# Transposing attention outputs and mask rows by DMA in place of TensorE, in a fused attention and MoE kernel

## The chip, the cores and the metric

The kernel runs on one core of one Trainium2 chip. The metric is the device time of one execution in microseconds (us). The profile is one further execution, and its span is about 1.7 us shorter than the time that the same execution is given. Engine names in the profile: PE is TensorE (matmuls and transposes), PEld its weight loads, DVE is VectorE, ACT is ScalarE, POOL is GpSimd, SP is SyncE, which here only issues DMAs.

## The reference

Four batches of eight heads, sequence 768, head dimension 64. Each query attends causally to its own block of 64 keys and to the best-scoring other blocks (gate: query times the mean key of a block). The concatenated heads then go through two dense layers with a tanh-approximated GELU.

```python
k_rep = k.reshape(B, H, n_blocks, block, D).mean(axis=3)
gate_scores = np.einsum('bhsd,bhnd->bhsn', q, k_rep)          # causal blocks only
top_idx = np.argsort(gate_scores, axis=-1)[..., -3:]          # plus the own block -> mask
attn = softmax(where(mask & causal, scale * q @ k.T, -1e9)) @ v
x = attn.transpose(0, 2, 1, 3).reshape(B * S, H * D)          # 3072 x 512
out = gelu_tanh(x @ w_in) @ w_out                             # 512 -> 2048 -> 512
```

## The kernel before

Two heads form a pair; there are 16 pairs, 4 to a batch. For each pair a preparation stage turns K and Q into columns (on PE for pairs 0 to 4, on DVE from pair 5 on), computes the gate, selects blocks, and writes mask rows under the Q columns. The head stage then computes scores, exponentials and the product with V. Each batch ends with two dense products: `s1` (w_in, then GELU) and `s2` (w_out).

The order of the instructions on every engine is fixed when the kernel is built: a planner in the kernel simulates the engines with guessed durations and writes the instructions down in the order that comes out. It decides the order only; at run time semaphores (counters that one engine raises and another waits for) decide the moment.

```python
# guesses: {engine: us}; "DMA" is the time a load takes to land, SP the issue
go = add({SP: 0.2}, emit_t if dve else emit, [free_sd.get(...)], prio=10 * p)
ld[key, p] = add({"DMA": 4.5 if dve else 2.0}, lambda _: None, [go, at_least], ...)

# mask rows of a pair: madd[i] is [128, 10, 32]: 5 query chunks x 2 heads, 32 columns each;
# one transpose takes one chunk of both heads (128 x 64)
def mask(_):
    mk16 = plan.buf["mk", p].bitcast(FP16)
    for c in range(1, NC):                                   # NC = 6
        nc.tensor.transpose(
            mk16[0:64, c * 128:(c + 1) * 128],
            madd[i][:, 2 * (c - 1):2 * c, :].rearrange("p a b -> p (a b)"), ident16)
m = add({PE: 0.27 * slow}, mask, [sel], pr, takes=("pre", ("mk", p)))
# ... then two copies of 12 x 640 from PSUM into qT16[i][h][64:76, 128:S] (DVE or ACT)

# output of a pair: six 128x128 transposes on PE, then a copy PSUM -> xT
def ot_e(_):
    oT16 = plan.buf["oT", p].bitcast(FP16)
    for c in range(NC):
        nc.tensor.transpose(
            oT16[:, c * 128:(c + 1) * 128],
            T["xn", p][:, c].rearrange("p h d -> p (h d)"), ident16)
ot = add({PE: 0.32 * slow}, ot_e, norms, base + 50, takes=("pre", ("oT", p)))

# 110 idle matmuls of lowest priority that keep PE warm in the first batch
z = const.tile([128, 512], FP16)
nc.vector.memset(z, 0.0)
for n in range(110):
    def emit(_, n=n):
        nc.tensor.matmul(plan.buf["warm", n][:, 0:256], z[:, 0:128],
                         z[:, 0:256], start=True, stop=True)
    add({PE: 0.107}, emit, [], 1e6, ...)
```

The softmax here doesn't subtract the row's maximum and nothing guards it: scores larger than these inputs give would overflow.

## Time and profile before

| | before |
|---|---|
| median time | 294.3 us |
| span of the profile | 291.4 us |
| PE busy | 279.3 us |
| first w_in matmul of batch 0 | 49.8 us |
| from there to the end of the span | 241.6 us |

The profiled execution took 293.1 us, 1.2 us under the median, and the table's last rows belong to it.

From the page of the kernel before: the span, the busy time of each engine, two rows of the span in 40 slices (tenths busy), and the engines of the chain of work that ended last.

```profile
span 291.4 us, 5960 instructions
...
PE 279.3 (96%) x2330; PEld 173.8 (60%) x2330; DVE 144.0 (49%) x448; ACT 191.5 (66%) x252; POOL 48.0 (16%) x119
...
PE   7998899899999999999999999999999999999994
...
DMA  9999999999999966865822110200000101100111
...
PE 80%; ACT 13%; DVE 3%; issue 2%; POOL 1%; ACTq 0%; DVEq 0%
```

PE is busy nearly everywhere and is 80% of the chain. The DMA engines are full for the first 14 of 40 slices and nearly idle in the second half. To see how tight PE is after the first batch, here are the busy times by stretch (start:end, length, busy, number of instructions, granted clock, DMA share, GB/s):

```profile
core 0: us, PE busy (x), PEclk, DMA share, GB/s
49.80:287.50 237.70, 235.34 (x1867) 1.00 0.45 84
119.00:146.00 27.00, 26.82 (x180) 1.00 0.71 126
```

From the first w_in matmul to the end of the last w_out product PE idles 2.4 us of 237.7. PE time that is taken out there should come off the span, unless something new makes PE wait. This is from the list of the w_in line's instructions (durations ns min/median/max, first and last start in us):

```profile
L629 PE MATMUL wide_85<-xT_555,w_in_102 x64: 270/324/390, 49.8 to 73.7; 128*128 128x512 f16 x32, 128*128 128x256 f16 x32
...
L629 PE MATMUL wide_86<-xT_3108,w_in_102 x64: 272/326/379, 247.2 to 266.6; 128*128 128x512 f16 x32, 128*128 128x256 f16 x32
```

What the two kinds of transposes take is read from the timeline of PE (start, duration, engine, line). The durations overlap, because matmuls are pipelined, so the cost of a group is the distance between its start and the next group's start. First a mask, then an output:

```profile
136.28 0.49 PE L629 MATMUL wide_86<-xT_1428,w_in_102 128*128 128x512 f16 x2
136.70 0.47 PE L472 MATMUL bank_88<-ident_96,madd_121 128*64 128x128 f16 x5
137.10 1.15 PE L629 MATMUL wide_86<-xT_1428,w_in_102 128*128 128x512 f16 x6
```

```profile
229.51 0.50 PE L600 MATMUL bank_88<-ident_96,xn_3219 128*128 128x128 f16 x6
229.85 0.38 PE L571 MATMUL bank_89<-v_126,at_0_1_3261 128*128 128x65 f16 x7
```

The mask group takes 0.40 us to the next start. In front of it another 0.1 us is lost: w_in matmuls in a row take 1.30 us for eight (in the list of the chain), so the two ahead should need 0.325 us, and the gap is 0.42. The output group takes 0.34 us.

### The profile page before, as it was taken

How to read it: one execution, taken by the hardware profiler on the slowest of the kernel's cores; microseconds unless marked ns; L12 is line 12 of the kernel's file. 1: busy time of each engine (PE TensorE's matmuls, PEld its weight loads, DVE VectorE, ACT ScalarE, POOL GpSimd, SP SyncE). 2: the span in 40 equal slices, each digit the busy share in tenths (PEclk: the TensorE clock that was granted, in tenths of full speed). 3: DMA queues.
4: the chain of work that ended last, by engine and by line, in shares of the span. 5: the costliest groups of instructions: out<-in, count | busy, mean ns of one | idle time of the engine just before them, and what ended most of it. 6: DMA issues, size and time to landing. Idle time of an engine off the chain costs nothing.

```text
span 291.4 us, 5960 instructions
## 1 busy us (share of the span) xinstructions
PE 279.3 (96%) x2330; PEld 173.8 (60%) x2330; DVE 144.0 (49%) x448; ACT 191.5 (66%) x252; POOL 48.0 (16%) x119
## 2 busy tenths in 40 slices
PE   7998899899999999999999999999999999999994
PEld 6776667575666655656646665666557644665441
DVE  4787873138578878673676978850024410000000
ACT  3667869557799695676789976376799921664111
POOL 7023224000043220000024430000034400000000
PEclk9999999999999999999999999999999999999999
DMA  9999999999999966865822110200000101100111
GB/s 171 219 213 197 190 171 174 199 170 146 168 159 175 163 133 146 177 127 97 128 43 64 58 38 37 74 0 0 2 36 2 40 36 72 38 0 2 72 72 72
DMA packets 115836, 29.75 MB, mean 102 GB/s; under 512 B 110176, under 2 KB 112224, under 8 KB 115808
## 3 DMA queue, kind: packets, MB, share of 16 engines
q1 hardware_dynamic: 113216, 25.18, 47.7%
q0 software_dynamic: 2592, 4.19, 8.4%
q8 instruction: 18, 0.29, 0.4%
q14 instruction: 10, 0.08, 0.1%
HBM read 27.26 MB, written 6.29 MB: 115 GB/s over the span
## 4 chain that ended last, share of the span: by engine, by line
PE 80%; ACT 13%; DVE 3%; issue 2%; POOL 1%; ACTq 0%; DVEq 0%
PE wide_86 L629 14%; PE wide_85 L629 14%; PE bank_88 L659 7%; PE bank_87 L659 7%; PE bank_90 L659 6%; PE bank_89 L659 6%; PE wide_85 L533 5%; PE wide_86 L533 4%; PE bank_89 L430 3%; PE bank_90 L571 2%; PE bank_89 L571 1%; PE bank_90 L430 1%; PE bank_88 L430 1%; PE bank_87 L571 1%; PE bank_88 L600 1%
## 5 line engine op out<-in xcount | busy, mean ns | idle before, releaser
L629 PEld LDWEIGHTS <-w_in_102 128*128 128x128 f16 x512 | 49.7, 99 | 34.0 <-issue 1.8
L659 PEld LDWEIGHTS <-gT_3446 128*128 128x128 f16 x96 | 9.4, 98 | 11.2
L659 PEld LDWEIGHTS <-gT_2781 128*128 128x128 f16 x96 | 9.1, 97 | 8.0
L694 PEld LDWEIGHTS <-z 128*128 128x128 f16 x110 | 10.9, 105 | 4.2 <-DVE bmask L164 1.3
L659 PEld LDWEIGHTS <-gT_1883 128*128 128x128 f16 x96 | 8.8, 98 | 7.6
L629 PE MATMUL wide_85<-xT_555,w_in_102 128*128 128x512 f16 x64 | 12.4, 326 | 1.0 <-ACT gT_986 L642 0.6
L629 PE MATMUL wide_86<-xT_1428,w_in_102 128*128 128x512 f16 x64 | 12.4, 326 | 0.2 <-ACT gT_1883 L642 0.2
L659 PEld LDWEIGHTS <-gT_986 128*128 128x128 f16 x96 | 8.5, 98 | 6.7
L629 PE MATMUL wide_85<-xT_3108,w_in_102 128*128 128x512 f16 x64 | 12.2, 326 | 0.0
L629 PE MATMUL wide_86<-xT_555,w_in_102 128*128 128x512 f16 x64 | 12.2, 326 | 0.0
L629 PE MATMUL wide_86<-xT_2319,w_in_102 128*128 128x512 f16 x64 | 12.0, 326 | 0.0
L629 PE MATMUL wide_85<-xT_2319,w_in_102 128*128 128x512 f16 x64 | 11.9, 326 | 0.0
L629 PE MATMUL wide_86<-xT_3108,w_in_102 128*128 128x512 f16 x64 | 11.7, 326 | 0.0
L629 PE MATMUL wide_85<-xT_1428,w_in_102 128*128 128x512 f16 x64 | 11.7, 326 | 0.0
L504 ACT ACT_TABLE_LOAD x8 | 10.3, 1283 | 0.9 <-PEq L746 0.8
L642 ACT ACTIVATE gT_986<-wide_85 128x768 f16<-128x768 f32 x8 | 6.5, 810 | 5.2 <-PE wide_85 L629 5.2
L190 DVE COPY osb_0_3000<-bank_89 128x512 f32<-128x512 f32 x1 | 0.7, 692 | 18.4 <-PE bank_89 L659 18.4
L659 PE MATMUL bank_90<-w_out_103,gT_2781 128*128 128x512 f16 x32 | 9.7, 379 | 0.0
L642 ACT ACTIVATE gT_986<-wide_86 128x768 f16<-128x768 f32 x8 | 6.5, 808 | 4.6 <-PE wide_86 L629 4.6
L694 PE MATMUL bank_88<-z 128*128 128x256 f16 x33 | 8.9, 290 | 0.3 <-ACT kT_1_107 L188 0.3
L642 ACT ACTIVATE gT_2781<-wide_86 128x768 f16<-128x768 f32 x8 | 6.5, 810 | 3.8 <-PE wide_86 L629 3.8
L642 ACT ACTIVATE gT_3446<-wide_86 128x768 f16<-128x768 f32 x8 | 6.5, 810 | 3.7 <-PE wide_86 L629 3.7
(947 smaller groups left out, 697.4 us busy)
## 6 DMA issues: line engine op xcount, KB each, us to landing
w_in_102<-in_moe_w_in_dram POOLq DMA_DIRECT2D x1, 2048.0 KB, 14.3
w_out_103<-in_moe_w_out_dram POOLq DMA_DIRECT2D x1, 2048.0 KB, 17.3
k_sd_135<-in_k_dram SPq DMA_DIRECT2D x2, 192.0 KB, 3.0
q_sd_142<-in_q_dram SPq DMA_DIRECT2D x2, 192.0 KB, 3.7
v_sd_147<-in_v_dram SPq DMA_DIRECT2D x2, 192.0 KB, 4.3
k_sd_152<-in_k_dram SPq DMA_DIRECT2D x2, 192.0 KB, 4.6
q_sd_157<-in_q_dram SPq DMA_DIRECT2D x2, 192.0 KB, 4.6
v_sd_162<-in_v_dram SPq DMA_DIRECT2D x2, 192.0 KB, 4.5
```

The costliest lines, as they stand in the source:

```text
L190: nc.vector.tensor_copy(out=out, in_=in_)
L430: nc.tensor.matmul(gt[:, (c - 1) * 24:c * 24], T["qT32", p][:, c * 128:(c + 1) * 128], T["ksb", p].rearrange("p h n -> p (h n)"), start=Tr ...
L504: nc.scalar.activation(out=t, in_=bmask[:, 0, 0:1], func=AF.Exp if key[0] == "exp" else AF.Gelu_apprx_tanh, bias=0.0, scale=1.0)
L533: nc.tensor.matmul(st[:, x:e], kT16[i][h][0:76, s0:s0 + 128], qT16[i][h][0:76, s0 + (x - cb):s0 + (e - cb)], start=True, stop=True)
L571: nc.tensor.matmul(pvv[:, qc, 0:65], at[:, cb + (qc - jc) * 128: cb + (qc - jc + 1) * 128], v16[i][:, jc, h, :], start=(gi == 0 and jc == ...
L600: nc.tensor.transpose(oT16[:, c * 128:(c + 1) * 128], T["xn", p][:, c].rearrange("p h d -> p (h d)"), ident16)
L629: nc.tensor.matmul(hps[:, u:e], w_in16[:, ci, f * 128:(f + 1) * 128], T["xT", b][:, ci, u:e], start=(ci == 0), stop=(ci == HP - 1))
L642: nc.scalar.activation(out=T["gT", b][:, f, :], in_=plan.buf["hps", b, f][:, 0:S], func=AF.Gelu_apprx_tanh, bias=0.0, scale=1.0)
L659: nc.tensor.matmul(plan.buf["ops", b, ti], T["gT", b][:, f, ti * 128:(ti + 1) * 128], w_out16[:, f, :], start=(f == 0), stop=(f == NF - 1))
L694: nc.tensor.matmul(plan.buf["warm", n][:, 0:256], z[:, 0:128], z[:, 0:256], start=True, stop=True)
```

## The change

The intent: PE is the bottleneck and the DMA engines are idle in the second half, so let them do the transposes. Output transposes go to DMA from pair 6 on (10 pairs), mask transposes from pair 8 on (8 pairs). Earlier pairs, in the stretch where the loads fill the DMA engines, stay on PE. The mask tile doubles to 64 columns per head, so that a chunk of both heads is a block of 128x128, and the two heads' mask rows come out at partitions 0 and 64 (before: 0 and 32). To make room, one kT32 buffer and two constant tiles go, and the warm-up matmuls take the identity matrix in place of a zeroed tile. The core of the diff:

```diff
-        madd.append(persist.tile([128, NG, 32], FP16, name=f"madd_{i}"))
+        madd.append(persist.tile([128, NG, 64], FP16, name=f"madd_{i}"))
...
+    def by_xbar(p):
+        return p >= 2 * HP                     # HP = 4: pair 8 on
...
+            T["E16"] = E16 = E32[0:12].bitcast(FP16)[:, 0:S]   # E32 is a kT32 buffer
...
-                    mk16[0:64, c * 128:(c + 1) * 128],
+                    mk16[:, c * 128:(c + 1) * 128],
...
+        def mask_dma(_):
+            T["mT", p] = hd.tile([128, S - 128], FP16, tag="mT", name=f"mT_{p}")
+            nc.sync.dma_start_transpose(
+                out=T["mT", p].rearrange("p (c q) -> p c q", q=128),
+                in_=madd[i].rearrange("p g n -> p (g n)"))
+        if by_xbar(p):
+            go = add({SP: 0.1}, mask_dma, [sel], pr)
+            m = add({"XBAR": 2.5}, lambda _: None, [go], pr)
+        else:
+            m = add({PE: 0.27 * slow}, mask, [sel], pr, takes=("pre", ("mk", p)))
...
+            nc.sync.dma_start_transpose(
+                out=T["xT", b][:, hp, :].rearrange("p (c q) -> p c q", q=128),
+                in_=T["xn", p].rearrange("p c h d -> p (c h d)"))
+        if p >= HP + 2:                        # pair 6 on
+            go = add({SP: 0.1}, ot_dma, norms, base - 20)
+            xts.setdefault(b, []).append(
+                add({"XBAR": 2.5}, lambda _: None, [go], base - 20))
...
-        z = const.tile([128, 512], FP16)
-        nc.vector.memset(z, 0.0)
+        z = ident16.unsqueeze(1).to_broadcast([128, 2, 128])
-                nc.tensor.matmul(plan.buf["warm", n][:, 0:256], z[:, 0:128], z[:, 0:256], ...)
+                nc.tensor.matmul(plan.buf["warm", n][:, 0:256], ident16, z, ...)
```

More of the change, by code (lines that the diff above doesn't have):

```diff
@@ L36 @@
     LAT = {"PE": 0.2, "ACT": 0.19, "DVE": 0.14, "POOL": 0.1, "SP": 0.1,
-           "DMA": 0.1, "NONE": 0.0}
+           "DMA": 0.1, "XBAR": 0.1, "NONE": 0.0}
     WINDOW = 0.03
@@ L148 @@
     hd = ctx.enter_context(tc.tile_pool(name="hd", bufs=3))
+    hd2 = ctx.enter_context(tc.tile_pool(name="hd2", bufs=2))
     atp = ctx.enter_context(tc.tile_pool(name="atp", bufs=7))
@@ L251, in e16 @@
         def e16(_):
-            T["E16"] = const.tile([12, S], FP16, name="E16")
-            E16 = T["E16"]
+            E32 = hd2.tile([128, S], FP32, tag="kT32", name="E32")
+            T["E16"] = E16 = E32[0:12].bitcast(FP16)[:, 0:S]
             nc.gpsimd.memset(E16, MASKVAL)
@@ L340, in emit @@
             def emit(_):
-                T[key + "T32", p] = hd.tile([128, S], FP32, tag=key + "T32",
-                                            name=f"{key}T32_{p}")
+                T[key + "T32", p] = (hd if key == "q" else hd2).tile(
+                    [128, S], FP32, tag=key + "T32", name=f"{key}T32_{p}")
                 nc.vector.transpose(
@@ L349, in pre @@
             t = add({DVE: 0.83}, tr("k"),
-                    [ld["k", p], last.get(p - 3, {}).get("pre")], pr)
+                    [ld["k", p], last.get(p - 2, {}).get("k32")], pr)
             free_sd["k", p] = t
@@ L392, in pre @@
         ksb = add({DVE: 0.1}, ksb_m, ksr, pr)
+        last.setdefault(p, {})["k32"] = add({"NONE": 0.0}, lambda _: None,
+                                            kcs + ksr, pr)
         def wq_t(a):
@@ L472, in mask @@
                 nc.tensor.transpose(
-                    mk16[0:64, c * 128:(c + 1) * 128],
+                    mk16[:, c * 128:(c + 1) * 128],
                     madd[i][:, 2 * (c - 1):2 * c, :].rearrange(
                         "p a b -> p (a b)"), ident16)
-        m = add({PE: 0.27 * slow}, mask, [sel], pr, takes=("pre", ("mk", p)))
         def mc(h):
             def emit(eng):
+                src = (T["mT", p] if by_xbar(p)
+                       else plan.buf["mk", p].bitcast(FP16)[:, 128:S])
                 copy(eng, qT16[i][h][64:76, 128:S],
-                     plan.buf["mk", p].bitcast(FP16)[
-                         32 * h:32 * h + 12, 128:S])
-            return emit
+                     src[64 * h:64 * h + 12, :])
+            return emit
+        def mask_dma(_):
+            T["mT", p] = hd.tile([128, S - 128], FP16, tag="mT",
+                                 name=f"mT_{p}")
+            nc.sync.dma_start_transpose(
[5 more added lines that the diff above has]
+        else:
+            m = add({PE: 0.27 * slow}, mask, [sel], pr,
+                    takes=("pre", ("mk", p)))
         mcs = [add({DVE: 0.4, ACT: 0.6}, mc(h), [m, old.get("s")], pr)
                for h in range(2)]
-        add({"NONE": 0.0}, lambda _: None, mcs, pr, gives=[("mk", p)])
+        add({"NONE": 0.0}, lambda _: None, mcs, pr,
+            gives=[] if by_xbar(p) else [("mk", p)])
         rdy[p] = [kcs[0::2] + [q16s[0], mcs[0], c_E["fill", i]],
@@ L602, in ot_e, with ot_dma @@
                     T["xn", p][:, c].rearrange("p h d -> p (h d)"), ident16)
+        def ot_dma(_):
+            if ("xT", b) not in T:
+                T["xT", b] = xtp.tile([128, HP, S], FP16, tag="xT",
+                                      name=f"xT_{b}")
+            nc.sync.dma_start_transpose(
[5 more added lines that the diff above has]
+                add({"XBAR": 2.5}, lambda _: None, [go], base - 20))
+            last.setdefault(p, {}).update(
+                {"k": st, "s": st, "v": pvs[-1]})
+            return
         ot = add({PE: 0.32 * slow}, ot_e, norms, base + 50,
@@ L689, in warm @@
     def warm():
-        z = const.tile([128, 512], FP16)
-        nc.vector.memset(z, 0.0)
+        z = ident16.unsqueeze(1).to_broadcast([128, 2, 128])
         for n in range(110):
             def emit(_, n=n):
-                nc.tensor.matmul(plan.buf["warm", n][:, 0:256], z[:, 0:128],
-                                 z[:, 0:256], start=True, stop=True)
+                nc.tensor.matmul(plan.buf["warm", n][:, 0:256], ident16, z,
+                                 start=True, stop=True)
             add({PE: 0.107}, emit, [], 1e6, takes=("warm", ("warm", n)),
```

## The prediction

> **What bounds the kernel now.** TensorE (PE). The page gives PE 279.3 us busy of a 291.4 us span, and the chain that ended last is 80% PE and 13% ScalarE. Read by stage (busy time of each engine in each stretch): from 56 to 287.6 us PE is busy 230.3 of 231.6 us, so it hardly ever waits there; VectorE and ScalarE have room (about half and two thirds busy). Wherever the attention heads wait for ScalarE's exponentials, the second MoE product (w_out) of the previous batch fills PE, and that filler is never used up: it ends at 118.7, 185.5 and 247 us, while the last head of each batch is normalised at about 112.8, 173.5 and 234.3 us. So PE time taken out after about 56 us should come off the span almost one for one; waits shorter than the filler cost nothing. Before 56 us the chain is VectorE, ScalarE and loads, and PE runs warm-up matmuls.
>
> **What is removed, from the timeline of PE.** An output transpose (6 transposes) takes 0.34 us from its first start to the next instruction (229.51 to 229.85). Ten pairs: 3.4 us. A mask transpose (5) takes 0.40 us (136.70 to 137.10) plus about 0.1 us before its first weight load ("issue" gaps of 0.3 us on the weight-load row), so 0.5 us. Eight pairs: 4.0 us. The mask pairs that stay get 128 columns in place of 64; their weight loads (110 ns against 98 ns for 128 columns) and that gap may shrink: 4 x 0.1 = 0.4 us after 56 us. Sum: 7.8 us, all on the PE chain. Also gone are ten PSUM copies of 0.56 us (VectorE) or 0.80 us (ScalarE), and PSUM bank holds; off the chain, so worth little.
>
> **What is added.** 18 DMA transposes of 160 to 192 KB on the SP queue. Plain transfers of 96 to 192 KB here take 2.9 to 4.5 us to land. The Trainium skill (VectorE: DVE Perf Modes, "The three transpose paths") gives 1309 ns for a 128x128 transpose through the DMA crossbar; six blocks in one DMA I estimate at 3 to 8 us with that page's figure. No run here shows it yet. Masks have over 10 us of slack: they are made a stage before the heads that use them. Outputs of pairs 11 and 15 have 12 to 13 us of filler. The tight one is pair 7: its xT is needed about 6 us after its normalisation, at 99% DMA share (DMA row, 76 to 119 us). I allow 0.7 us for a stall there and for reshuffled static order. The third kT32 buffer that goes, and the memset of a wider mask tile, should stay hidden.
>
> **Prediction.** 294.3 - 7.8 + 0.7 = 287.2 us, range 285.0 to 290.5. Faster by over 2% (below 288.4): 0.68; within 2%: 0.29; slower: 0.03.
>
> **What would show each step right.** PE instructions fall by 100 (2330 to 2230) and PE busy time by some 7 us; PE still over 96% busy from 56 us on; no output transposes on PE after batch 0 but for pairs 4 and 5; the DMA transposes land within 8 us; the first w_in matmul of batch 1 waits under 1 us for xT. The w_in stretches start progressively earlier: by about 2 us at the third, 7 us at the fourth.
>
> **What would make it wrong.** DMA transposes of 10 us and more, so that w_in matmuls wait for xT; transposes waiting in the SP queue behind output stores or loads (or holding loads up behind them); contention that delays loads between 76 and 144 us; a static order of instructions, planned with 2.5 us per transpose, that is unlucky where the real latency differs; warm-up or first-batch work that starts later.

## More of the kernel before

The start of the kernel turned out to matter. Its timeline (all engines):

```profile
1.30 0.39 PE L694 MATMUL bank_87<-z 128*128 128x256 f16 x1 [1.30 <-DVE bmask L164]
...
2.04 0.91 DVE L161 CAST ident_96<-ident_91 128x128 f16<-128x128 f32 x1 [0.65 <-POOL ident_91 masks.py:199]
...
5.36 0.49 PE L313 MATMUL bank_90<-ident_91,k_sd_135 128*128 128x128 f32 x3
```

The zeroed tile (its memset starts at 0.97 us) is ready early. The identity, which GpSimd and VectorE prepare, is cast only by 2.95 us (2.04 + 0.91). The first warm-up matmul starts at 1.30 us, and 23 of them stand ahead of the first K transpose on PE's queue.

## The result, and the profile after

| | before | after |
|---|---|---|
| median time | 294.29 us | 287.25 us |
| runs | 294.07 to 294.37 | 286.02 to 288.27 |
| ratio | | 0.976 (95% interval 0.972 to 0.980) |

Ratios are the mean time of one kernel's fast runs over that of the other's fast runs of the same rounds, so not quite the ratio of the medians. The change is faster by 2.4%. The runs of the changed kernel spread over 2.2 us, those of the kernel before over 0.3 in these rounds (0.9 to 1.4 in later ones). The profile below is of the slowest of the four runs of the changed kernel, and the profile before is of a fast one, so the two spans differ by 4.9 us where the medians differ by 7.0.

The page of the changed kernel, same lines:

```profile
span 286.5 us, 5770 instructions
...
PE 271.4 (95%) x2230; PEld 169.7 (59%) x2230; DVE 141.7 (49%) x442; ACT 186.6 (65%) x247; POOL 48.6 (17%) x119
...
PE   5988988899999999998999999999999999999994
...
DMA  9999999999997886897872536313011321000111
...
PE 79%; ACT 6%; DVE 6%; DMA 4%; issue 2%; POOL 1%; SPq 0%; ACTq 0%; DVEq 0%; POOLq 0%
```

PE lost 100 instructions and 7.9 us of busy time. The DMA row is fuller in the second half. DMA has entered the chain with 4%. Busy time by stretch, from the first w_in matmul and for the w_in stretch of batch 1:

```profile
core 0: us, PE busy (x), PEclk, DMA share, GB/s
52.50:282.70 230.20, 226.79 (x1767) 1.00 0.53 99
119.00:146.00 27.00, 25.48 (x160) 1.00 0.87 142
```

PE now idles 3.4 us in its main stretch, 1.5 of them between 119 and 146 us, where it idled 0.2 before. The w_in line of the changed kernel:

```profile
L665 PE MATMUL wide_88<-xT_556,w_in_105 x64: 270/324/381, 52.5 to 76.3; 128*128 128x512 f16 x32, 128*128 128x256 f16 x32
...
L665 PE MATMUL wide_89<-xT_3033,w_in_105 x64: 272/326/379, 242.4 to 261.8; 128*128 128x512 f16 x32, 128*128 128x256 f16 x32
```

Batch 0's w_in product begins 2.7 us **later** than before (52.5 against 49.8), the last batch's 4.8 us earlier. So the stretch from the first w_in matmul to the end of the span fell from 241.6 us to 234.0, by 7.6 us, and the start gave part of that back. The transposes' landing, from the list of DMA issues:

```profile
xT_1429<-xn_1724 SPq DMA_TRANSPOSE x1, 2.8
mT_1834<-madd_112 SPq DMA_TRANSPOSE x1, 3.8
mT_1932<-madd_118 SPq DMA_TRANSPOSE x1, 4.0
```

The last columns are the count and the us to landing. Over all 18, masks land 2.4 to 4.2 us after the issue, outputs 2.7 to 4.4. The plan had 2.5. In the Trainium skill (VectorE: DVE Perf Modes, "The three transpose paths") one 128x128 transpose by DMA takes 1309 ns; here five or six of them in one DMA land after some 3 us, so well under that figure for each.

Two places lose time. The first is the start (timeline, all engines):

```profile
2.05 0.91 DVE L162 CAST ident_99<-ident_94 128x128 f16<-128x128 f32 x1 [0.83 <-POOL ident_94 masks.py:199]
...
3.01 0.39 PE L729 MATMUL bank_90<-ident_99 128*128 128x256 f16 x1 [3.01 <-DVE ident_99 L162]
...
7.89 0.77 PE L317 MATMUL bank_93<-ident_94,k_sd_136 128*128 128x128 f32 x3
```

The warm-up matmuls now wait for the identity, which GpSimd makes and VectorE casts by 3.0 us. The first K transpose stands behind 23 of them and starts at 7.89 us in place of 5.36. The second is the batch-1 w_in stretch, again in the timeline of all engines:

```profile
126.38 0.28 DVE L463 SCALAR_TENSOR_TENSOR madd_118<-sel_1918,ownm_195 128x120 f16<-128x120 f32 x1
...
127.09 1.52 SPq L495 DMA_TRANSPOSE mT_1932<-madd_118  x1
...
131.13 0.72 ACT L189 COPY qT_1_114<-mT_1932 12x640 f16<-12x640 f16 x1 [1.20 <-DMA mT_1932<-madd_118]
131.13 0.32 DVE L191 COPY qT_0_113<-mT_1932 12x640 f16<-12x640 f16 x1 [3.58 <-DMA mT_1932<-madd_118]
...
133.46 0.70 PE L665 MATMUL wide_88<-xT_1429,w_in_105 128*128 128x512 f16 x3 [1.14 <-ACT gT_1865 L678]
```

The mask of pair 9 is written by 126.7 us, issued at 127.1 and lands at 131.1. VectorE has its mask copy next in order and stands still for 3.58 us; ScalarE has the other copy ahead of GELUs, so these come late and PE waits 1.14 us for one. No score of pair 9 is computed before 154 us, so nothing needed this mask soon. What needed the engines was the work queued behind the copies.

### The profile page after: what moved, and what is told of

The parts are those of the page before. It is cut to its first block, busy times and chain, and to the rows that moved or that the text cites. A ratio compares the mean times of both kernels' runs of the same rounds, so it can differ in the third digit from the quotient of the medians.

```text
span 286.5 us, 5770 instructions
## 1 busy us (share of the span) xinstructions
PE 271.4 (95%) x2230; PEld 169.7 (59%) x2230; DVE 141.7 (49%) x442; ACT 186.6 (65%) x247; POOL 48.6 (17%) x119
## 4 chain that ended last, share of the span: by engine, by line
PE 79%; ACT 6%; DVE 6%; DMA 4%; issue 2%; POOL 1%; SPq 0%; ACTq 0%; DVEq 0%; POOLq 0%
PE wide_88 L665 13%; PE wide_89 L665 13%; PE bank_90 L695 8%; PE bank_92 L695 8%; PE bank_91 L695 7%; PE wide_88 L554 6%; PE wide_89 L554 5%; PE bank_93 L695 3%; PE bank_93 L592 2%; PE bank_93 L437 2%; PE bank_92 L437 2%; PE bank_91 L437 2%; PE bank_90 L592 1%; DMA mT_1932<-madd_118 1%; DMA mT_1834<-madd_112 1%
## 5 line engine op out<-in xcount | busy, mean ns | idle before, releaser
L665 PEld LDWEIGHTS <-w_in_105 128*128 128x128 f16 x512 | 50.0, 99 | 35.4 <-issue 2.8
L695 PEld LDWEIGHTS <-gT_3363 128*128 128x128 f16 x96 | 9.4, 98 | 11.2
L729 PEld LDWEIGHTS <-ident_99 128*128 128x128 f16 x110 | 11.4, 109 | 5.8 <-DVE ident_99 L162 3.0
L695 PEld LDWEIGHTS <-gT_2720 128*128 128x128 f16 x96 | 9.1, 97 | 8.2
L695 PE MATMUL bank_92<-w_out_106,gT_987 128*128 128x512 f16 x48 | 13.6, 379 | 0.0
L695 PEld LDWEIGHTS <-gT_1865 128*128 128x128 f16 x96 | 9.0, 98 | 7.5
L665 PE MATMUL wide_88<-xT_556,w_in_105 128*128 128x512 f16 x64 | 12.4, 325 | 1.0 <-ACT gT_987 L678 0.6
L665 PE MATMUL wide_88<-xT_1429,w_in_105 128*128 128x512 f16 x64 | 11.9, 325 | 1.1 <-ACT gT_1865 L678 1.1
L695 PEld LDWEIGHTS <-gT_987 128*128 128x128 f16 x96 | 8.7, 99 | 6.8
L665 PE MATMUL wide_88<-xT_3033,w_in_105 128*128 128x512 f16 x64 | 12.2, 326 | 0.0
L665 PE MATMUL wide_89<-xT_556,w_in_105 128*128 128x512 f16 x64 | 12.2, 326 | 0.0
L665 PE MATMUL wide_88<-xT_2290,w_in_105 128*128 128x512 f16 x64 | 12.0, 325 | 0.0
L665 PE MATMUL wide_89<-xT_3033,w_in_105 128*128 128x512 f16 x64 | 11.7, 326 | 0.0
L665 PE MATMUL wide_89<-xT_1429,w_in_105 128*128 128x512 f16 x64 | 11.7, 326 | 0.0
L665 PE MATMUL wide_89<-xT_2290,w_in_105 128*128 128x512 f16 x64 | 11.7, 326 | 0.0
L525 ACT ACT_TABLE_LOAD x8 | 10.3, 1283 | 0.9 <-PEq L781 0.8
L729 PE MATMUL bank_90<-ident_99 128*128 128x256 f16 x24 | 7.2, 308 | 3.1 <-DVE ident_99 L162 3.0
L678 ACT ACTIVATE gT_987<-wide_88 128x768 f16<-128x768 f32 x8 | 6.5, 811 | 5.1 <-PE wide_88 L665 4.9
L678 ACT ACTIVATE gT_2720<-wide_88 128x768 f16<-128x768 f32 x8 | 6.5, 810 | 5.0 <-PE wide_88 L665 5.0
L695 PE MATMUL bank_91<-w_out_106,gT_2720 128*128 128x512 f16 x32 | 9.7, 379 | 0.0
L695 PE MATMUL bank_91<-w_out_106,gT_1865 128*128 128x512 f16 x32 | 9.7, 379 | 0.0
L678 ACT ACTIVATE gT_987<-wide_89 128x768 f16<-128x768 f32 x8 | 6.5, 809 | 4.7 <-PE wide_89 L665 4.7
```

What stands on the lines that cost most here:

```text
L525: nc.scalar.activation(out=t, in_=bmask[:, 0, 0:1], func=AF.Exp if key[0] == "exp" else AF.Gelu_apprx_tanh, bias=0.0, scale=1.0)
L665: nc.tensor.matmul(hps[:, u:e], w_in16[:, ci, f * 128:(f + 1) * 128], T["xT", b][:, ci, u:e], start=(ci == 0), stop=(ci == HP - 1))
L678: nc.scalar.activation(out=T["gT", b][:, f, :], in_=plan.buf["hps", b, f][:, 0:S], func=AF.Gelu_apprx_tanh, bias=0.0, scale=1.0)
L695: nc.tensor.matmul(plan.buf["ops", b, ti], T["gT", b][:, f, ti * 128:(ti + 1) * 128], w_out16[:, f, :], start=(f == 0), stop=(f == NF - 1))
L729: nc.tensor.matmul(plan.buf["warm", n][:, 0:256], ident16, z, start=True, stop=True)
```

## The experiments

Twelve kernels ran. Each was correct against the reference. Times are medians of four runs; ratios are to the kernel before in the same rounds. Two theories to begin with. A: the identity-fed warm-up delays the whole first batch. B: the plan's 2.5 us for a transpose puts the mask copies too early on DVE and ACT. The rival to A is that loads hide the late start; the rival to B is that a different static order only moves waits.

### e1_zero_warm: the changed kernel with a zeroed warm-up tile

```diff
-        z = ident16.unsqueeze(1).to_broadcast([128, 2, 128])
+        zt = const.tile([128, 128], FP16, name="zt")
+        nc.vector.memset(zt, 0.0)
+        z = zt.unsqueeze(1).to_broadcast([128, 2, 128])
-                nc.tensor.matmul(plan.buf["warm", n][:, 0:256], ident16, z,
+                nc.tensor.matmul(plan.buf["warm", n][:, 0:256], zt, z,
```

> The changed kernel, with its warm-up matmuls again fed by a zeroed tile of their own (one memset of 128x128) in place of the identity. Theory A: the identity is ready only at 3.0 us (against 1.3 us for the zeroed tile), so the 23 warm-up matmuls ahead of the first K transpose on PE start later and run slow longer, and all of batch 0 is late by 2 to 3 us: then the first K transpose starts at about 5.4 us in place of 7.9, the first w_in matmul at about 49.7 in place of 52.4, and the time falls by 2 to 3 us from the changed kernel's (to about 284.5 to 285.5). Rival: batch 0 is bound by loads, so the late start is absorbed before the first w_in matmul and the time moves under 0.7 us.

Measured: 285.6 us, ratio 0.972, so 1.65 us below the changed kernel's median (of other rounds; by the ratios it is 0.4%, 1.2 us). The first K transpose starts at 5.34 us and the first w_in matmul at 49.6. The rest of the span, 234.1 us, is the same as in the changed kernel (234.0). So the edit acts on the start alone. Theory A holds against its rival (under 0.7 us), but the gain is below the 2 to 3 us expected, which were read from two profiles: the profile of the changed kernel was its slowest run.

### e2_plan_4p5: the changed kernel planned with 4.5 us per transpose

```diff
-            m = add({"XBAR": 2.5}, lambda _: None, [go], pr)
+            m = add({"XBAR": 4.5}, lambda _: None, [go], pr)
-                add({"XBAR": 2.5}, lambda _: None, [go], base - 20))
+                add({"XBAR": 4.5}, lambda _: None, [go], base - 20))
```

> The changed kernel, planned with 4.5 us in place of 2.5 us for each DMA transpose (only the static order changes). Theory B: VectorE stood 3.6 us at the mask copy of pair 9 because the mask landed after 4.0 us where 2.5 were planned; that held up ScalarE's gelu and then PE (PE busy 1.86 us of the 3.0 us from 131 to 134). Ordering for the real latency takes this away: PE idle between the first w_in matmul of batch 1 and the last of it falls by about 1.5 us, time by 1 to 2 us from the changed kernel's. Rival: the waits only move elsewhere and the time stays within 0.5 us.

Measured: 285.3 us, ratio 0.970, 2.0 us below the changed kernel's median (1.6 us by the ratios). Busy time of PE in the two stretches (batch 1's w_in product; first w_in matmul to the end of the last w_out product):

```profile
119.00:146.00 27.00, 27.00 (x176) 1.00 1.00 158
51.60:279.80 228.20, 226.49 (x1767) 1.00 0.56 101
```

No idle time is left from 119 to 146 us, and the stretch from the first w_in matmul to the end of the span is 232.0 us in place of 234.0. PE's idle time in its main stretch fell from 3.41 to 1.71 us. Theory B holds; no wait of PE took the place of the one removed. VectorE still waits 5.9 us in all for masks, but PE does not wait for what comes after. One order was tried against one: other planned values, which would give other orders, were not.

### e3_both: both edits

> Both edits: zeroed warm-up tile and 4.5 us planned. If theories A and B hold and add up, 3 to 5 us below the changed kernel: about 282.5 to 284. If the rivals hold, about 287.

Measured: 283.5 us, ratio 0.9645 (0.9625 to 0.9665). The first w_in matmul is at 49.4 us and 231.9 us follow. The two edits add up. **This version beats both kernels**: 10.3 us below the kernel before, 3.8 us below the changed one.

### e4_before_ident: the kernel before with identity-fed warm-up

```diff
-        z = const.tile([128, 512], FP16)
-        nc.vector.memset(z, 0.0)
+        z = ident16.unsqueeze(1).to_broadcast([128, 2, 128])
-                nc.tensor.matmul(plan.buf["warm", n][:, 0:256], z[:, 0:128], z[:, 0:256], ...)
+                nc.tensor.matmul(plan.buf["warm", n][:, 0:256], ident16, z, ...)
```

> The kernel before, with only its warm-up matmuls fed by the identity, as the change does. Theory A: 2 to 3 us slower than before (about 296.5 to 297), first w_in matmul at about 52 us in place of 49.7. Rival (absorbed by loads): within 0.7 us of before.

Measured: 295.8 us against 293.8 in the same rounds, ratio 1.0054. The first w_in matmul is at 51.4 us, and the rest is 241.7 us as before (241.6). This is theory A alone in the other kernel: 1.6 us by the ratio and 2.0 by the medians for a tile of zeros, just below what was expected.

The first K transpose starts at 7.0 to 7.9 us in the three profiles with an identity-fed warm-up (the changed kernel, e2, e4) and at 5.1 to 6.0 us in the six with a zeroed tile and as many warm-up matmuls ahead of it (before, e1, e3, e5, e6, e7). So the edit separates the two groups, and within each the start varies by 0.8 to 0.9 us. The timelines show what varies with it. Before, PE issues warm-up matmuls every 0.21 us from 1.30 to 4.5 us and every 0.11 us after that; in the profile of the changed kernel they still come every 0.21 us when the weight loads of the K transposes begin at 7.7 us, 4.7 us after the first. The Trainium skill (TensorE: Matmul & The Clock Gate, Part 1) says that the array runs at half rate until a free-running window of about 3.4 us has been busy. The 3.2 us before are a little under that figure; the 4.7 us exceed it, as they would if the matmuls began just after a window had. That this phase makes the 2.2 us of spread in the changed kernel's runs is argued, not shown.

### e7_no_dma_transpose, e5_outputs_only, e6_masks_only: one part at a time

All three are e3_both with transposes put back on PE:

```diff
 e7, e5:  -        return p >= 2 * HP        +        return p >= NPAIR     # masks
 e7, e6:  -        if p >= HP + 2:           +        if p >= NPAIR:        # outputs
```

> e3_both with every transpose back on PE: what is left of the change is the mask tile of 64 columns per block pair (PE transposes of 128x128 in place of 128x64), two kT32 buffers, and the shared E tile. Theory C: the wider tile alone pays, because a group of five wide mask transposes occupies PE for 0.28 us (69.83 to 70.11 in the changed kernel's timeline) where the narrow group took 0.49 us; 12 groups after 56 us give 2.5 us. So about 291.3 us (0.9915 of before). Rival (the prediction's view): the width is worth 0.4 us in all, and the ratio is 0.997 to 1.

> e3_both with the masks of all pairs on PE (wide); outputs by DMA from pair 6 on. Theory C: eight wide groups of 0.28 us come back, 2.3 us: ratio 0.9645 + 0.008 = 0.972. The prediction's view (0.5 us a group): 4 us come back, 0.978.

> e3_both with all outputs transposed on PE; masks by DMA from pair 8 on. Ten groups of 0.34 us come back, 3.4 us: ratio 0.9645 + 0.0116 = 0.976. If the PSUM copies and bank holds that return matter too, 0.98 or more.

Measured, with e3_both and the kernel before for comparison. The third column is the span less the first w_in matmul's start; the fourth is PE's idle time from that start to the end of the last w_out product.

| kernel | median, ratio | after the first w_in matmul | PE idle there |
|---|---|---|---|
| before | 293.6 to 293.8, 1 | 241.6 us | 2.4 us |
| e7 (no DMA transposes) | 291.3, 0.992 | 239.5 us | 2.6 us |
| e5 (outputs by DMA) | 287.5, 0.978 | 235.4 us | 2.5 us |
| e6 (masks by DMA) | 287.8, 0.980 | 235.8 us | 1.6 us |
| e3 (both by DMA) | 283.5, 0.9645 | 231.9 us | 1.7 us |

The rows before and e3 have profiles from other rounds. The medians of e5 and e6 also hold a later start: their first w_in matmul came at 50.6 us, that of e3 at 49.4. The third column leaves the start out, and it adds up. Outputs by DMA: 4.1 us without the masks (239.5 to 235.4), 3.9 with them (235.8 to 231.9). Masks by DMA: 3.7 and 3.5 us. And 2.1 us come without any DMA transpose, in e7, where theory C said 2.5 (the ratio's interval, 0.989 to 0.996, leaves out the rival's 0.997 to 1). The saving is visible in the changed kernel's timeline of PE, at a mask group that stayed on PE:

```profile
69.50 0.49 PE L665 MATMUL wide_88<-xT_556,w_in_105 128*128 128x512 f16 x2
69.83 0.44 PE L479 MATMUL bank_93<-ident_99,madd_112 128*128 128x128 f16 x5
70.11 1.14 PE L665 MATMUL wide_88<-xT_556,w_in_105 128*128 128x512 f16 x6
```

Five transposes of 128x128 take 0.28 us to the next start and nothing is lost ahead of them (69.50 to 69.83 is what the two matmuls need). The narrow group took 0.40 + 0.1. All 12 wide groups after the first w_in matmul in e7 take 0.28 us, and all 12 narrow ones before 0.39 to 0.40. A transpose with twice the columns is cheaper. The Trainium skill (TensorE: Matmul & The Clock Gate, "Weight-path perf modes") says that the fast weight load is on when the number of weights is 128 and the type is not FP32; a stationary operand of 64 columns misses that. The trace agrees in the direction: the loads are 106 to 110 ns each for 64 columns and 95 to 101 ns for 128. But some 10 ns for each of five loads are only 0.05 of the 0.21 us. The timelines show one more difference: the first narrow load starts together with its transpose (both at 136.70 us, after 0.32 us without a load), the first wide one 0.11 us ahead of it (69.72 and 69.83), under the matmul before. That the width saves time is shown; why is not. Twelve groups after the first w_in matmul, 0.21 us each, are 2.5 us; 2.1 are seen. e7 also has two kT32 buffers and the shared E tile, which were not tried apart.

In e5 theory C missed: wide mask groups on PE should cost 8 x 0.28 = 2.3 us and the ratio was that of 4 us. In the timeline of e5 the groups do take 0.28 us. Of the rest, 0.8 to 0.9 us is PE idle time that the masks on PE bring (2.5 against 1.7 us); about 0.4 us is not accounted for. For the outputs, 10 x 0.34 = 3.4 us was expected and 4.0 came; 0.6 us stays open.

### e8_from_pair_4: DMA transposes in the load-heavy stretch too

```diff
-        return p >= 2 * HP
+        return p >= HP
-        if p >= HP + 2:
+        if p >= HP:
```

> e3_both with outputs and masks by DMA from pair 4 on, so also in the load-heavy stretch. Theory D: with transposes planned at 4.5 us nothing there is worse than in the light stretch; PE loses 2 output groups (0.68 us) and 4 mask groups (1.1 us): 1.8 us faster, ratio 0.9585. Rival (the change's own reason for leaving them on PE): between 56 and 110 us, at a DMA share near 1, the transposes land after 6 us or more, stall VectorE at the mask copies or hold the SP queue up, and the time is the same as e3_both or worse.

Measured: 299.9 us, ratio 1.020, 16 us worse than e3_both. Theory D fell, and so did the first reason of its rival, slow landing: the 24 transposes landed 2.4 to 4.4 us after their issue. What the rival named beside it came: VectorE stood at mask copies, because the issue was late. SP's queue (timeline):

```profile
67.06 3.60 SPq L221 DMA_DIRECT2D q_sd<-in_q_dram  x4
70.75 3.43 SPq L221 DMA_DIRECT2D k_sd<-in_k_dram  x4
74.29 2.75 SPq L221 DMA_DIRECT2D q_sd<-in_q_dram  x4
...
78.31 1.31 SPq L495 DMA_TRANSPOSE mT<-madd  x1
```

VectorE's side of it:

```profile
66.75 0.28 DVE L463 SCALAR_TENSOR_TENSOR madd<-sel,ownm 128x120 f16<-128x120 f32 x1
...
82.10 0.32 DVE L191 COPY qT<-mT 12x640 f16<-12x640 f16 x1 [12.39 <-DMA mT<-madd]
```

The mask of pair 4 was written at 67.0 us. SP was then issuing loads, 2.75 to 3.6 us for four of 96 KB, and reached the transpose at 78.3. The plan gave each such load 0.2 us of SP. VectorE stood 12.4 us. PE ran out of work, and then ran slower:

```profile
60.00:70.00 10.00, 10.00 (x69) 1.00 1.02 165
70.00:80.00 10.00, 3.81 (x24) 0.85 0.90 138
80.00:90.00 10.00, 6.29 (x24) 0.50 1.02 151
```

(Columns: start:end, length, PE busy, instructions, granted clock, DMA share, GB/s.) After some 6 us with little work the granted clock was 0.50 in the next stretch, so even the work that came was slow. The load traffic is not cleared of a part in this: in the changed kernel such a four-part load holds SP for 2.6 to 3.8 us between 65 and 90 us and for 2.0 to 2.9 us from 95 us on, so the issue itself is longer where loads are dense.

### e10_pair4_sp_planned and e9_sp_planned: planning SP's issue time

Theory E: the time is lost in the SP queue. e10 is e8 and e9 is e3_both with these edits:

```diff
-        go = add({SP: 0.2}, emit_t if dve else emit,
+        go = add({SP: 2.3 if dve else 1.1}, emit_t if dve else emit,
-        ... add({"DMA": 4.5 if dve else 2.0}, ...
+        ... add({"DMA": 3.0 if dve else 2.0}, ...
-            go = add({SP: 0.1}, mask_dma, [sel], pr)
+            go = add({SP: 1.25}, mask_dma, [sel], -100)
-            go = add({SP: 0.1}, ot_dma, norms, base - 20)
+            go = add({SP: 1.25}, ot_dma, norms, -100)
-            {"XBAR": 4.5} twice,  add({SP: 0.1}, out_e, ...)
+            {"XBAR": 3.2} twice,  add({SP: 0.4}, out_e, ...)
```

> e8_from_pair_4 with the SP queue planned at what its issues took (loads 2.3 and 1.1 us, transposes 1.25, stores 0.4, in place of 0.2, 0.1 and 0.1) and transposes put first when SP is free; landing 3.2 us after the issue. Theory E: e8 lost because a ready mask waited in the SP queue behind the issues of five loads (ready at 67.0 us, issued at 78.3), not because it landed late (median 2.6 us); planned so, the long waits of VectorE and ScalarE for mask copies go (from 17 and 13 us to under 4 each), and the time returns to 282 to 284. Rival: the load-heavy stretch itself is the cause (contention on the DMA engines), and the time stays above 290.

> e3_both (outputs from pair 6, masks from pair 8) with the same SP plan. Its remaining VectorE waits for masks are 5.9 us in sum but PE has little idle time left (1.6 us between 56 and 206), so at most 1 us: 282.5 to 284. If the new static order is worse for the loads, up to 286.

Measured: e10 294.8 us (1.003), e9 294.2 us (1.0025). e10 is 5 us better than e8 and far from the forecast (it stays above 290, the number of theory E's rival); e9 is 10.7 us worse than e3_both. More true numbers made a worse plan. VectorE still waited 20 us for masks in e10 and 9.6 in e9, though the masks landed within 4.2 us of their issue. In e9's timeline one mask was ready at 119.7 us and was issued at 122.5, behind a load and a store on SP, and VectorE stood 5.4 us. The loads are crowded: from 100 to 140 us the DMA share is 1.28 in e9 and 1.20 in e10, 0.92 in e3_both, with SP issuing almost without a break; from 145 to 155 us it is 0.00 in both, 0.26 in e3_both. The edits changed five guesses and two priorities at once, so which of them crowded the loads is not known. What is shown: this plan, with durations of SP nearer the truth, did not mend it.

### e12_pair4_on_act: the transposes issued from ScalarE's queue

```diff
-            nc.sync.dma_start_transpose(      # both places
+            nc.scalar.dma_start_transpose(
-            go = add({SP: 0.1}, ...)          # both, with "XBAR" 4.5
+            go = add({ACT: 1.25}, ...)        # both, with "XBAR" 3.2
```

> e8_from_pair_4 with all 24 DMA transposes issued from ScalarE's queue in place of SP's (planned as 1.25 us of ScalarE and 3.2 us to land); loads and stores stay on SP. Theory E (a ready mask stood in the SP queue behind load issues; the transposes themselves land in time also among the loads): the pair-4 mask is issued within 2 us of being ready, PE's long wait in the batch-0 w_in stretch (9.9 us in e8) falls under 2 us, no drop of the granted clock there, and the time comes to 281 to 286, depending on what 24 issues of 1.2 us cost ScalarE. Rival (traffic of the load-heavy stretch): the transposes land after 6 us or more there, waits of 5 us and more remain, the time stays above 290.

Measured: 305.4 us, ratio 1.042, the slowest of all and above 290 as the rival said. Yet the part that theory E was about came out as said. The mask of pair 4, written at 67.7 us, was issued at 67.9, and PE stayed busy where e8 had lost it (columns as for e8):

```profile
70.00:80.00 10.00, 9.82 (x62) 1.00 0.55 77
...
110.00:120.00 10.00, 6.63 (x32) 0.66 1.23 214
```

From 70 to 80 us PE is busy 9.82 us, where e8 had 3.81. But this mask took 5.8 us to land, and later PE starves, as from 110 to 120 us, where the granted clock fell to 0.66. The list of what SP's queue waited for, between 60 and 130 us (us in total, times, longest):

```profile
SPq L211 <- DMA mT<-madd: 14.1, 2, 8.6
SPq L221 <- DMA mT<-madd: 10.3, 2, 5.2
SPq L221 <- DMA xT<-xn: 5.2, 1, 5.2
```

The loads on SP waited some 30 us in all (14.1 + 10.3 + 5.2) for transposes issued from the other queue. What released a wait is inferred in these lists, but SP's own times fit: two groups of loads, begun at 67.05 and 74.72 us, held it for 7.57 and 7.14 us, each until just after a mask had landed. The source asks for no such wait, and the lists of the kernels with loads and transposes both on SP (the changed kernel, e3, e8, e9, e10) show none. So one jam (masks behind loads) became another (loads behind masks). That the second is what makes e12 slower than e8 is argued: no run has the one without the other. The Trainium skill (DMA: Bandwidth & Descriptors, "Issuing engines are not separate DMA queues") says that issuing from several engines only saves the sequencer's time to issue, which is usually small beside the transfer. For one DMA the trace agrees: in e8 a load of 96 KB took SP 0.52 us and landed after 3.4 us (medians). But four of them in a row held SP for 2.2 to 3.6 us, and a mask that stood behind several such loads waited for the sum.

What e8, e10 and e12 settle: leaving pairs 4 to 7 on PE is better than any of three ways tried to move them, and late issue, not a late landing, is what e8 shows at its first stall. Whether another arrangement of the queues could make the early pairs pay stays open.

### e11_warm_planned: fewer warm-up matmuls ahead of the first K transpose

```diff
-            add({PE: 0.107}, emit, [], 1e6, ...
+            add({PE: 0.213 if n < 15 else 0.107}, emit, [], 1e6, ...
```

> e3_both with the first 15 warm-up matmuls planned at the 0.213 us that they take cold, in place of 0.107, so that fewer stand ahead of the first K transposes on PE. If what remains of the start is bound by them, the first K transpose starts at about 4.4 us in place of 5.1 and the time falls by 0.5 to 0.8 us; if by loads, within 0.3 us of e3_both (283.5).

Measured: 283.4 us, ratio 0.9646, the same as e3_both (0.9645). The first K transposes in its timeline:

```profile
4.54 1.51 PE L317 MATMUL bank<-ident,k_sd 128*128 128x128 f32 x6 [0.71 <-DMA k_sd<-in_k_dram]
```

They start 0.6 us earlier than in e3_both, now waiting for the load, but the six take 1.5 us in place of 0.8: fewer warm-up matmuls went ahead (12), and PE is still at the slow pace. Nothing was gained this way.

## Why the prediction was right

The time was forecast at 287.2 us and measured at 287.25. The mechanism was right, and the hit to 0.05 us is luck: the gain and the losses were both undersized, and the two errors nearly cancelled.

- *PE bounds the kernel after 56 us and removed PE time comes off one for one.* Right. PE is 98.6% busy from 56 to 283 us in the changed kernel (223.8 of 227.0 us), and the column of remaining time in the table of parts falls with what is taken off PE.
- *Outputs 3.4 us, masks 4.0 us.* Outputs were a little undersized: 4.0 us. Masks: 3.6 us against wide groups on PE (e7 to e6, e5 to e3); against the narrow groups of before, which the 4.0 us were read from, a part of e7's 2.1 us comes on top.
- *Wider masks save 0.1 us a group, 0.4 us in all.* Undersized by half per group: 0.21 us (0.49 to 0.28). Done for all pairs, with no DMA transpose, this part of the change was worth 2.1 us.
- *Pair 7's output is the tight one.* It was not. It was issued at 114.9 us, landed 2.8 us later, and its consumer began at 119.4 with no wait.
- *Masks have over 10 us of slack.* This is the step that failed. The heads that consume a mask do come much later, but the copy that moves it sits in a fixed order on VectorE and ScalarE, and whatever is behind it waits too. This cost 1.6 to 2.0 us (e2, by ratios and by medians), over twice the 0.7 us allowed for stalls of all kinds.
- *Warm-up that starts later* was named among the risks and given no number. It cost 1.2 to 2.0 us (e1 and e4, by ratios and by medians), and could be read from the diff: the identity in the trace of before is ready at about 3.0 us, the zeroed tile at 1.3.
- *The third w_in stretch earlier by 2 us, the fourth by 7.* In the profiles 2.1 (dense w_in work from 186.3 to 184.3; two matmuls of it were put at 179.4) and 4.8 (247.2 to 242.4). The second is 2.2 us short of the forecast, less than the 2.7 us by which that profile starts late.

- *Plain transfers land in 2.9 to 4.5 us; six blocks by DMA transpose in 3 to 8.* The first holds (up to 4.6) for loads issued after about 62 us; some earlier ones took up to 15 us. The transposes landed after 2.4 to 4.4 us, at the low end or under it.

In sum, by the ratios the change with both faults mended (e3) is worth 10.4 us, where 7.8 were forecast; in the profiles 9.7 of them lie after the first w_in matmul (241.6 to 231.9). The change as made lost 3.4 us of it where 0.7 were forecast, and 7.0 were left against 7.1.

## What to carry to other kernels

When work moves to a DMA, ask not only when its result is needed, but which instruction of an in-order engine waits for it, and what stands behind that instruction; here planning with the slowest landing seen (4.5 us), not a typical one, removed the wait. Look at the small parts of a diff as closely as at its purpose: a warm-up operand and a tile's width each moved as much here as the output transposes of three to five pairs (0.4 us a pair). A queue that issues many small loads is itself an engine with a busy time, so count it before giving it something urgent; e9 and e10 show that putting those times into the plan is not by itself a cure.

## What the Trainium skill lacked or had wrong

- VectorE: DVE Perf Modes, "The three transpose paths": this section gives 1309 ns for one 128x128 transpose by DMA and no time for several in one DMA; what other pages say of such transposes is a bandwidth, not a time to landing. Here five blocks landed 2.4 to 4.2 us after the issue and six blocks 2.7 to 4.4 us (changed kernel), also while loads filled the DMA engines (e8: 2.4 to 4.4). The prediction's estimate from that page was 3 to 8 us.
- DMA: Bandwidth & Descriptors, "Issuing engines are not separate DMA queues": the time to issue is called usually small beside the transfer. It is for one load of 96 KB (0.52 us against 3.4 to landing, e8), but nothing is said of the sum in one queue: a four-part load of 4 x 96 KB in runs of 128 bytes took SP 2.2 to 3.6 us, a DMA transpose of 160 to 192 KB held it 1.2 us as a rule and up to 2.4, and SP's queue delayed a ready transpose by 11.3 us (e8).
- DMA: Bandwidth & Descriptors, "Rules for kernel authors" says "A transpose next to ordinary DMAs needs nothing". With the transposes on one queue and the loads on another, the built program nevertheless had the loads' queue wait for the transposes, some 30 us in all between 60 and 130 us (e12). No page warns of this cost; whether the chip needs the wait or only the build put it there, no run shows.
- TensorE: Matmul & The Clock Gate, Part 4, gives some 275 to 390 ns for a PE transpose of 128x128. Each lasts about 0.22 us in these profiles, but in a row they overlap and take PE 0.056 us each (0.28 us for five, 0.34 for six). That a transpose of 64 columns costs more than one of 128 (0.49 against 0.28 us for five) is not said there; the page's section on weight loads gives a reason that the load times here (106 to 110 against 95 to 101 ns) cover only in part.
